# Weight parts of a feed-forward stage: low halves by accumulating DMA, no copies of parts in HBM, weight loads from GpSimd's queue

## The chip, the cores and the metric

The kernel runs on one core of one Trainium2 chip. The metric is the device time of one execution in microseconds (us). A core has five engines that run side by side and wait for one another through semaphores: TensorE (PE in the profile; its weight loads are PEld), VectorE (DVE), ScalarE (ACT), GpSimd (POOL) and SyncE (SP). SP computes nothing here; it issues DMAs. POOL computes and can also issue DMAs on a queue of its own. TensorE's clock is granted by a throttle, and the profile shows the granted share.

## The reference, cut to what matters

```python
x: (1, 2048, 512);  H = 32 heads of Dh = 16;  window W = 8, dilation 2;  F = 1792
qkv = x @ wqkv                                  # (512, 1536)
logits[s, w] = q[s] . k[s - 2*w] / 4            # masked where s - 2*w < 0
a = (sum over w of softmax(logits) * v[s - 2*w]) @ wo
b = (gelu(x @ w_gate) * (x @ w_up)) @ w_down    # (512, 1792) twice, (1792, 512)
g = sigmoid(sum(x * gate_w))
out = g * a + (1 - g) * b
```

Everything is float32.

## The kernel before

**Parities and stages.** Because the dilation is 2, even and odd tokens never meet in the attention. The 2048 tokens are two parities (`par`) of 1024 tokens, each of two blocks of 512. TensorE first does the projections to q, k, v of both parities (`project`, three blocks of columns `cb`). Then comes the feed-forward part of parity 0 (`ffn(0)`), 14 chunks `f` of 128 hidden channels, its end (`finish(0)`: the output projection with `wo`, added to the feed-forward sums, and the output), and then the same for parity 1. The sliding attention is VectorE's work: a generator (`attention`) yields it in small pieces, and `pull(budget)`, called between TensorE's products, takes as many pieces as the budget pays for. An attention unit is 128 channels of one parity, 8 in all; each has 8 pieces of scores (L238, L239), a softmax and 8 pieces of mixing (L273, L277, L278, L279).

**Two parts per operand.** TensorE takes the rounded type fp32r. To keep float32's precision each operand is a high part (the value rounded by a ScalarE copy) and a low part (value minus high part), and each product is three matmuls: high by high, high by low, low by high. `split` (L64 to L69) makes both parts: L68 on ScalarE, L69 a subtraction on VectorE or GpSimd.

**Seven products in place of eight.** `gate_up` computes gate and up of two token blocks with a Strassen-like scheme: seven products of sums. The x operands are a11, a12, a22 and the sums s1 to s4 (`sums`); the weight operands are b11, b21, b22 and the differences t1 to t4 (`combine`, three VectorE subtractions a chunk, L344). `product` is six matmuls of 128x512 (L381), so 42 a chunk; `down` multiplies hidden activations by `w_down` (L420), six matmuls a piece, 16 pieces for each pair of chunks. VectorE adds two products to saved copies (L390), multiplies gate by up (L394) and, in parity 0, makes the low part of the hidden activations (L397); in parity 1 GpSimd makes that.

**Where the weight parts come from.** In parity 0, `fetch` loads a chunk's raw weights from SP's queue, `combine` forms t1 to t4, and `operands` splits each of the seven 128x256 operands: high on ScalarE, low on GpSimd. Each pair of parts is also written to HBM (`WS`), and parity 1 only reads them back. `down_w` does the same with `w_down` (tiles `d`, HBM copies `DS`). `operands(f + 1)` is advanced a step at a time (`idle`, `next(more)`) while chunk f computes.

**The x operands of parity 1** are made at the end of `ffn(0)` (`operands_1`): x is loaded again, and ScalarE and GpSimd split a11, a12, a22 and the four sums.

**Order.** A scheduler with a timeline of its own fixes, when the program is built, the order of the instructions on each engine; on the chip each engine runs its list in that order.

The kernel lays its HBM scratch for the attention's output (`OS`) so that `channels` reads it with four DMAs of 64 KB per half unit.

Of the kernel before, what the change touches and what calls it, by code (L numbers as in the profile page):

```python
# [16 lines left out]
P = 128  # L17
# [16 lines left out]
OPS = ("b11", "t1", "t2", "b21", "b22", "t3", "t4")  # L34
# [3 lines left out]
def tile_gated_mix(ctx: ExitStack, tc: tile.TileContext, xt, wqkv, wff, wo, out):  # L38
# [6 lines left out]
    BUFS = {"A": 16, "S": 16, "w": 14, "d": 4, "raw": 2, "t": 1, "hh": 6, "hl": 6, "c": 4, "s": 3,  # L45
            "r": 2, "rt": 4, "p": 4, "lg": 2}
    COLS = {"w": 2 * WQ, "c": 2 * WQ, "d": 1024, "t": 1024, "raw": WT}

    def tl(tag, dt=F32):
        return pool.tile([P, COLS.get(tag, 512)], dt, name=tag, bufs=BUFS[tag])  # L50

# [20 lines left out]
    KS, VS, QS, OS, WS, DS = {}, {}, {}, {}, {}, {}  # L72
    for par in range(2):
# [6 lines left out]
        for u in range(NU):  # L80
            for half in range(2):
                OS[par, u, half] = dram.tile([32, 4, BT * P], F32, name=f"os{par}{u}{half}")


    early = iter(["c", "rt"] * 99)
    X, WC = {}, {}

    def load_xk(kc, blk, first=False):
        hi, lo = tl("A", F32R), tl("A", F32R)
        X[0, blk, kc] = hi, lo  # L90
        for a, n in ((0, P), (P, 512 - P)) if first else ((0, 512),):
            raw = tl(next(early))
# [4 lines left out]
    def load_cb(cb, kc, eng, tag=None):  # L97
        hi, lo = tl("w", F32R), tl("w", F32R)
        WC[cb, kc] = hi, lo
        raw = tl(tag or "c")  # L100
        if cb == 1:
            n = 2 * WQ
            for hh in range(2):
                nc.sync.dma_start(raw[:, hh * WQ:(hh + 1) * WQ], wqkv[hh, 2, :, kc * WQ:(kc + 1) * WQ])
        else:
            n = 512
            nc.sync.dma_start(raw[:, :n], wqkv[cb // 2, kc // 2, :, kc % 2 * 512:kc % 2 * 512 + 512])
        return lambda: split(eng, hi[:, :n], lo[:, :n], raw[:, :n])

    def sums(par, kc, a, b, eng, put, eng2=None):  # L110

        t = tl("t")
        s1, s2, s3, s4 = t[:, :512], t[:, 512:], b[:, :512], a[:, 512:1024]
        eng.tensor_tensor(s1, b[:, :512], b[:, 512:1024], op=OP.add)
        eng.tensor_tensor(s2, s1, a[:, :512], op=OP.subtract)
        eng.tensor_tensor(s3, a[:, :512], b[:, :512], op=OP.subtract)
        eng.tensor_tensor(s4, a[:, 512:1024], s2, op=OP.subtract)
        for n, s in (("s1", s1), ("s2", s2), ("s4", s4), ("s3", s3)):
            hi, lo = tl("S", F32R), tl("S", F32R)
            split(eng2 or eng, hi, lo, s)  # L120
            put(n, hi, lo)
            yield

    def raw_pair(par, kc):
        ab = []
        for blk in range(2):
            raw = tl("raw")
            nc.sync.dma_start(raw[:, :1024].rearrange("p (a c) -> p a c", a=2), xt[2 * par + blk, :, kc:kc + 3:2, :])
            ab.append(raw)
        return ab  # L130

    XOP, nxt = {}, {}

    def load_x1():
        for kc in range(2):
            a, b = raw_pair(1, kc)
            for blk, raw in ((0, a), (1, b)):
                for i in range(2):
                    if blk == 1 and (kc, i) != (1, 1):
                        d = tl("d", F32R)  # L140
                        hi, lo = d[:, :512], d[:, 512:]
                    else:
                        hi, lo = tl("hh", F32R), tl("hl", F32R)
                    X[1, blk, kc + 2 * i] = hi, lo
                    split(nc.vector, hi, lo, raw[:, i * 512:(i + 1) * 512])

    def operands_0():
        for kc in range(2):
            a, b = raw_pair(0, kc)
            for _ in sums(0, kc, a, b, nc.vector, lambda n, hi, lo: XOP.__setitem__((n, kc), (hi, lo))):  # L150
                pass
# [3 lines left out]
    def operands_1(first):  # L155
        for kc in range(2):
            a, b = raw_pair(1, kc) if kc else first
            for n, raw in (("a11", a[:, :512]), ("a12", a[:, 512:1024]), ("a22", b[:, 512:1024])):
                nxt[n, kc] = tl("A", F32R), tl("A", F32R)
                split(nc.gpsimd, *nxt[n, kc], raw)  # L160
                yield
            yield from sums(1, kc, a, b, nc.vector, lambda n, hi, lo: nxt.__setitem__((n, kc), (hi, lo)), nc.gpsimd)
# [100 lines left out]
    def mix(par, u):  # L263
# [4 lines left out]
        tb = pool.tile([P, NP, UC], F32, name="tb")  # L268
        for jj in range(NP):
            if jj % BT == 0:  # L270
                o = pool.tile([P, BT, UC], F32, name="o")
# [7 lines left out]
            nc.vector.tensor_tensor(o[:, jj % BT], prod[:, 0], prod[:, 1], op=OP.add)  # L279
            yield 1.4  # L280

            if jj % BT == BT - 1:
                nc.vector.transpose(tb[:, jj + 1 - BT:jj + 1].rearrange("p t c -> p (t c)"),
                                    o.rearrange("p t c -> p (t c)"))
                for a in range(4):
                    nc.sync.dma_start(OS[par, u, jj // BT][:, a], tb[32 * a:32 * a + 32, jj + 1 - BT:jj + 1])
# [44 lines left out]
    RAW = {}  # L331

    def fetch(f):
        raw = tl("raw")
        nc.sync.dma_start(raw[:, :1024], wff[f, :, :1024])
        RAW[f] = [raw]

    def combine(f):

        raw, t = RAW[f][0], tl("t")  # L340
        quart = raw[:, :1024].rearrange("p (a b) -> p a b", a=4)
        b11, b21, b12, b22 = (raw[:, i * 256:(i + 1) * 256] for i in range(4))
# [313 lines left out]
```

## Time and profile before

| what | value |
|---|---|
| three timed runs | 678.10, 679.92, 680.22 us; median 679.92 |
| profiled execution | 680.39 us; its span on the core is 678.6 us |
| busy, share of the span | PE 93%, PEld 76%, DVE 86%, ACT 46%, POOL 35% |
| matmuls | 2839 |
| mean granted clock of TensorE | 0.967 |
| DMA traffic | 136.46 MB, 201 GB/s over the span; SP's queue 63.8% of 16 engines' time, POOL's 0.1% |

How to read it: the profile is of one execution, 1.8 us longer than its span and within 0.1% of the median. Busy time counts instructions under way, waits left out. A row of groups such as "L277 DVE TENSOR_TENSOR ... x64 | 59.0, 922" says that 64 instructions of line 277 took 59.0 us together, 922 ns each on average. Matmuls overlap in the pipeline: in a full stretch they start every 0.227 us (88 in 20 us), though each is listed at about 0.4 us.

### The profile page before, as it was taken

Reading aid. Unit: us, or ns where it says so; the run is one execution under the profiler, and the core shown is the slowest. Engines: PE = TensorE matmul, PEld = TensorE weight load, DVE = VectorE, ACT = ScalarE, POOL = GpSimd, SP = SyncE. Lnnn points to the kernel's source line nnn. Section 1 sums busy time; section 2 is a strip of 40 time slices with the busy share of each in tenths; the row PEclk is TensorE's granted clock in tenths of the full one; section 3 lists DMA queues with packets and bytes.
Section 4 is the critical chain, followed back from the end, with each engine's and each line's share of the span. In section 5 each row is a group of like instructions: output and inputs, shape, how many; then the busy total and the mean of one; then the engine's idle time right before and its main releaser. Section 6 shows DMA issues by size and latency. Waiting matters only on the chain.

```text
span 678.6 us, 8894 instructions
## 1 busy us (share of the span) xinstructions
PE 631.2 (93%) x2839; PEld 512.9 (76%) x2839; DVE 584.4 (86%) x714; ACT 313.8 (46%) x601; POOL 236.1 (35%) x198
## 2 busy tenths in 40 slices
PE   8998999996799979997989849999999999999997
PEld 6888998874587758875868637888777888887785
DVE  5439899879999999989999988998999999989432
ACT  4424442245446455655454564234434644454562
POOL 5204014066737364634471760023122221224220
PEclk9999999998799989998998978999999999999999
DMA  8885755597966665675457587776566766544163
GB/s 254 269 253 172 247 156 187 172 300 250 310 235 218 243 229 171 234 252 208 156 191 224 159 225 158 249 234 218 179 187 197 214 196 197 185 124 127 36 104 124
DMA packets 116046, 136.46 MB, mean 201 GB/s; under 512 B 42400, under 2 KB 68640, under 8 KB 116000
## 3 DMA queue, kind: packets, MB, share of 16 engines
q1 hardware_dynamic: 115488, 135.84, 63.8%
q8 instruction: 22, 0.36, 0.2%
q14 instruction: 24, 0.20, 0.1%
q0 software_dynamic: 512, 0.07, 0.1%
HBM read 81.80 MB, written 54.07 MB: 200 GB/s over the span
## 4 chain that ended last, share of the span: by engine, by line
DVE 41%; PE 38%; DMA 7%; issue 6%; ACT 4%; SPq 1%; POOL 1%; DVEq 0%; POOLq 0%; ACTq 0%
PE p L381 21%; DVE prod L273 6%; PE p L420 6%; PE acc L420 5%; DVE prod L238 5%; DVE prod L277 4%; DVE lg L239 4%; DMA raw<-xt 4%; PE acc L557 3%; PE p L557 3%; DVE t L344 3%; DVE c L394 3%; DVE c L390 2%; DVE prod L278 2%; DVE o L279 2%
## 5 line engine op out<-in xcount | busy, mean ns | idle before, releaser
L381 PE MATMUL p<-S,w 128*128 128x512 f32 x672 | 176.6, 406 | 10.2 <-DVE c L390 4.1
L381 PEld LDWEIGHTS p<-S,w 128*128 128x128 f32 x672 | 130.8, 195 | 42.8 <-DVE c L390 4.5
L381 PE MATMUL p<-A,w 128*128 128x512 f32 x504 | 135.6, 407 | 16.2 <-DVE c L390 16.0
L381 PEld LDWEIGHTS p<-A,w 128*128 128x128 f32 x504 | 97.1, 194 | 42.4 <-DVE c L390 20.0
L397 POOL TENSOR_TENSOR hl<-c,hh 128x512 fp32r<-128x512 f32 x28 | 44.7, 1595 | 168.5 <-ACT hh L396 141.4
L238 DVE TENSOR_TENSOR prod<-k,q 128x1024 f32<-128x1024 f32 x64 | 86.8, 1356 | 11.5 <-DMA q<-qs 10.6
L273 DVE TENSOR_TENSOR prod<-v,lg 128x1024 f32<-128x1024 f32 x64 | 81.5, 1273 | 6.7 <-DMA v<-vs 5.3
L420 PE MATMUL p<-d,hh 128*128 128x512 f32 x224 | 71.7, 405 | 10.5 <-ACT p L414 10.4
L239 DVE TENSOR_REDUCE lg<-prod 128x64 f32<-128x1024 f32 x64 | 77.7, 1214 | 1.1
L69 POOL TENSOR_TENSOR w<-t,w 128x256 fp32r<-128x256 f32 x56 | 58.4, 1056 | 48.2 <-ACT w L68 38.5
L396 ACT ACTIVATE hh<-c 128x512 fp32r<-128x512 f32 x56 | 35.3, 631 | 80.3 <-DVE c L394 80.0
L69 POOL TENSOR_TENSOR w<-raw,w 128x256 fp32r<-128x256 f32 x42 | 43.0, 1034 | 63.8 <-ACT w L68 60.6
L277 DVE TENSOR_TENSOR prod<-prod 128x512 f32<-128x512 f32 x64 | 59.0, 922 | 1.3
L420 PEld LDWEIGHTS p<-d,hh 128*128 128x128 f32 x224 | 43.0, 194 | 22.0 <-ACT p L414 11.8
L420 PE MATMUL acc<-d,hh 128*128 128x512 f32 x224 | 57.7, 394 | 0.7 <-ACT hh L396 0.7
L420 PEld LDWEIGHTS acc<-d,hh 128*128 128x128 f32 x224 | 41.8, 188 | 11.7 <-ACT hh L396 2.4
L394 DVE TENSOR_TENSOR c<-c 128x512 f32<-128x512 f32 x56 | 44.6, 796 | 5.2 <-ACT c L482 4.8
L385 ACT ACTIVATE s<-p 128x512 f32<-128x512 f32 x56 | 32.8, 593 | 26.2 <-PE p L381 26.2
L390 DVE TENSOR_TENSOR c<-p,s 128x512 f32<-128x512 f32 x56 | 38.0, 681 | 8.0 <-PE p L381 7.8
L420 PE MATMUL p<-d,hl 128*128 128x512 f32 x112 | 42.9, 394 | 0.0
L429 ACT ACTIVATE rt<-p 128x512 f32<-128x512 f32 x48 | 28.6, 595 | 29.4 <-PE p L420 28.0
L177 PE MATMUL p<-w,A 128*128 128x512 f32 (+2 forms) x192 | 38.5, 345 | 2.9 <-ACT w L68 1.1
(125 smaller groups left out, 1002.0 us busy)
## 6 DMA issues: line engine op xcount, KB each, us to landing
ws<-w SPq DMA_DIRECT2D x98, 256.0 KB, 2.9
w<-ws SPq DMA_DIRECT2D x98, 256.0 KB, 2.7
raw<-wff SPq DMA_DIRECT2D x14, 512.0 KB, 5.0
ds<-d SPq DMA_DIRECT2D x14, 512.0 KB, 3.9
d<-ds SPq DMA_DIRECT2D x14, 512.0 KB, 4.5
raw<-xt SPq DMA_DIRECT2D x12, 512.0 KB, 5.4
k<-ks SPq DMA_DIRECT2D x8, 512.0 KB, 5.0
q<-qs SPq DMA_DIRECT2D x8, 512.0 KB, 6.3
```

Of the source, the lines that this page charges most:

```text
L69: eng.tensor_tensor(lo, raw, hi.bitcast(F32), op=OP.subtract)
L177: nc.tensor.matmul(ps[:, :cn], a[:, t], w[:, c0:c0 + cn], start=(kc == 0 and n == 0), stop=(kc == KC - 1 and n == 2))
L238: nc.vector.tensor_tensor(prod, k[:, jj:jj + W, :], q[:, jj, None, :].to_broadcast([P, W, UC]), op=OP.mult)
L239: nc.vector.tensor_reduce(lg[:, jj].rearrange("p w h -> p (w h)"), prod.rearrange("p w (h d) -> p (w h) d", d=DH), axis=AX.X, op=OP.add)
L273: nc.vector.tensor_tensor(prod.rearrange("p w (h d) -> p w h d", d=DH), v[:, jj:jj + W, :].rearrange("p w (h d) -> p w h d", d=DH), lg[:, ...
L277: nc.vector.tensor_tensor(prod[:, :4], prod[:, :4], prod[:, 4:], op=OP.add)
L381: nc.tensor.matmul(ps, w_, a_, start=(start and kc == 0 and n == 0), stop=(kc == 1 and n == 2), skip_group_check=True)
L390: nc.vector.tensor_tensor(c, ps, s, op=OP.add)
L394: nc.vector.tensor_tensor(ge, ge, up, op=OP.mult)
L397: eng.tensor_tensor(hl_, ge, hh_.bitcast(F32), op=OP.subtract)
L420: nc.tensor.matmul(pp, a[:, ts], w, start=(i == 0 and n == 0 and gr == 0), stop=(i == 1 and n == 2), skip_group_check=True)
L557: nc.tensor.matmul(pa, a, b, start=False, stop=(u == NU - 1 and n == 2), skip_group_check=True)
```

## The change

- `operands` no longer splits seven operands one by one. Raw weights and differences now lie side by side in one tile `raw` of eight quarters, in the order t1, t2, b11, b12, b22, t3, t4, b21, and are handled in two groups (t1, t2, b11: 768 columns; b22, t3, t4, b21: 1024 columns). For each group ScalarE writes the negated high part into the place of the low part, a DMA from GpSimd's queue adds the raw values onto it (`accum_op=OP.add`), and ScalarE writes the high part. This is done in both parities; `WS` and `DS` are gone, so parity 1 fetches raw weights, runs `combine` and splits `w_down` (on GpSimd) like parity 0.
- Weights, `w_down` and `wo` are loaded from GpSimd's queue; the outputs of parity 0 leave from it as well.
- The x operands of parity 1 are made at the beginning (`load_x1`): VectorE makes the sums and all the low parts, GpSimd's queue writes the parts to HBM (`keep`, 28 DMAs of 256 KB), and in the last chunk of parity 0 the queue reads them back (`operands_1`, 14 DMAs of 512 KB). `sums` works in place.
- `OS` is laid out so that one DMA reads a half unit in `channels`; VectorE's last addition of a mix piece writes `o` in another order.
- Buffers are regrouped (`g0`, `g1` for the weight parts, pairs in `A` and `S`).

```diff
+GROUPS = (("t1", "t2", "b11"), ("b22", "t3", "t4", "b21"))
+QUARTS = ("t1", "t2", "b11", "b12", "b22", "t3", "t4", "b21")
...
+    def keep(n, kc, hi, lo):
+        x = XS[n, kc] = dram.tile([P, 1024], F32, name=f"x{n}{kc}")
+        nc.gpsimd.dma_start(x[:, :512], hi.bitcast(F32))
+        nc.gpsimd.dma_start(x[:, 512:], lo.bitcast(F32))
     def load_x1():
...
+            for n, x in sums(a, b):
+                hi, lo = pair("S")
+                split(nc.vector, hi, lo, x)
+                keep(n, kc, hi, lo)
...
-    def operands_1(first):
+    def operands_1(n):
         for kc in range(2):
-            a, b = raw_pair(1, kc) if kc else first
-            for n, raw in (("a11", a[:, :512]), ("a12", a[:, 512:1024]), ("a22", b[:, 512:1024])):
-                nxt[n, kc] = tl("A", F32R), tl("A", F32R)
-                split(nc.gpsimd, *nxt[n, kc], raw)
-                yield
-            yield from sums(1, kc, a, b, nc.vector, lambda n, hi, lo: nxt.__setitem__((n, kc), (hi, lo)), nc.gpsimd)
+            t = tl("A" if n[0] == "a" else "S", F32R)
+            nc.gpsimd.dma_start(t.bitcast(F32), XS[n, kc])
+            XOP[n, kc] = t[:, :512], t[:, 512:]
...
-            nc.vector.tensor_tensor(o[:, jj % BT], prod[:, 0], prod[:, 1], op=OP.add)
+            two = [prod[:, i].rearrange("p (b c) -> p b c", b=4) for i in range(2)]
+            nc.vector.tensor_tensor(o[:, :, jj % BT], *two, op=OP.add)
...
     def fetch(f):
-        raw = tl("raw")
-        nc.sync.dma_start(raw[:, :1024], wff[f, :, :1024])
-        RAW[f] = [raw]
+        raw = RAW[f] = tl("raw")
+        r = raw.rearrange("p (a c) -> p a c", c=QW)
+        q = wff[f, :, :1024].rearrange("p (a c) -> p a c", c=QW)
+        nc.gpsimd.dma_start(r[:, 2::5], q[:, :2])
+        nc.gpsimd.dma_start(r[:, 3:5], q[:, 2:])
+    def fetch_d(f):
+        RD[f] = tl("r")
+        nc.gpsimd.dma_start(RD[f], wff[f, :, 1024:])
     def combine(f):
...
-        sub(t[:, :512].rearrange("p (a b) -> p a b", a=2), quart[:, 2:], quart[:, 0::2])
-        sub(t2, b22, t1)
-        sub(t4, b21, t2)
+        sub(r[:, 0:6:5], r[:, 3:5], r[:, 2:4])
+        sub(q["t2"], q["b22"], q["t1"])
+        sub(q["t4"], q["b21"], q["t2"])
-    def operands(par, f):
+    def operands(f):
...
-            if par:
-                nc.sync.dma_start(w[:, :512].bitcast(F32), WS[f][i])
-            else:
-                split(nc.gpsimd, w[:, :256], w[:, 256:512], RAW[f][n])
-                nc.sync.dma_start(WS[f][i], w[:, :512].bitcast(F32))
+            raw = RAW[f][:, (0, 4)[i] * QW:][:, :n]
+            nc.scalar.activation(lo, raw, AF.Copy, scale=-1.0)
+            nc.gpsimd.dma_start(lo.bitcast(F32), raw, accum_op=OP.add)
             yield
+            nc.scalar.activation(hi, raw, AF.Copy)
+            yield
-    def down_w(par, f):
+    def down_w(f):
         d = WD[f] = tl("d", F32R)
-        if par:
-            nc.sync.dma_start(d.bitcast(F32), DS[f])
-            return
-        rd = tl("r")
-        nc.sync.dma_start(rd, wff[f, :, 1024:])
-        DS[f] = dram.tile([P, 1024], F32, name=f"ds{f}")
-        split(nc.gpsimd, d[:, :512], d[:, 512:], rd)
-        nc.sync.dma_start(DS[f], d.bitcast(F32))
+        split(nc.gpsimd, d[:, :512], d[:, 512:], RD.pop(f))
...
     def channels(par, u, half):
         o = tl(("r", "rt")[half])
-        src = OS[par, u, half].rearrange("i a (t b j) -> b i (a t) j", t=BT, b=4)
-        for b in range(4):
-            nc.sync.dma_start(o[32 * b:32 * b + 32].rearrange("p (m j) -> p m j", j=32), src[b])
+        nc.sync.dma_start(o, OS[par, u, half].rearrange("b i a c -> (b i) (a c)"))
...
-                    nc.sync.dma_start(out_v[2 * jj + par, :, c], r[:, c])
+                    (nc.sync if par else nc.gpsimd).dma_start(out_v[2 * jj + par, :, c], r[:, c])
```

More of the change, by code (lines that the diff above doesn't have):

```diff
@@ L1 @@
 from contextlib import ExitStack
-from itertools import chain
 import numpy as np
@@ L110, in sums, with columns, of @@
[L110 to L121, printed above, removed]
-            yield
+    def columns():
+        def of(*tags):
+            for tag, n in tags:
+                t = tl(tag, F32R)
+                yield from (t[:, i * 2 * WQ:(i + 1) * 2 * WQ] for i in range(n))
+        cb0 = of(("g1", 4), ("g1", 4))
+        cb1 = of(("g0", 3), ("g0", 3), ("hh", 1), ("hl", 1))
+        for cols in (cb0, cb1):
+            for _ in range(KC):
+                yield next(cols), next(cols)
+        cols = of(("g1", 4))
+        for _ in range(2):
+            yield next(cols), next(cols)
+        yield pair("d")
+        yield tl("c", F32R), tl("c", F32R)
@@ L446, in piece, with anew @@
                 down(par, *s)
+        def anew(*names):
+            if not par and f == FC - 1:
+                for n in names:
+                    operands_1(n)
         X_ = bank("p")
@@ L484, in gate_up, with ahead, again @@
         late.append(last)
+    AGAIN = {}
+    def ahead():
+        combine(0)
+        AGAIN[0] = operands(0)
+        for _ in range(2):
+            yield next(AGAIN[0])
+    def again():
+        yield from AGAIN.pop(0)
+        yield from load_o((2, 3), (tl("c", F32R)[:, :512] for _ in range(4)))
+        fetch(1)
+        yield
+        combine(1)
     def ffn(par):
@@ L598, in tile_gated_mix @@
     combine(0)
-    ops = operands(0, 0)
-    for i in range(6):
-        next(ops)
+    for _ in operands(0):
+        pass
     combine(1)
```

197 lines of the change are left out of this document (120 added, 77 removed).

## The prediction

> **What bounds the kernel now.** I read the page first, then busy time by stage, then TensorE's waits, then the order of time on VectorE and GpSimd. The page gives TensorE 93% and VectorE 86%, but shares over the span mix stages, so I cut it at four points: the first feed-forward matmul (144), where the clock recovers and the end of parity 0 is under way (400), the first product of parity 1 (435.3), and the last mix of the attention (633.5).
>
> ```profile
> 144.00:400.00 256.00, 224.74 (x910) 177.54 (x908) 246.75 (x285) 133.51 (x268) 144.90 (x123) 0.94 0.67 222
> 400.00:435.30 35.30, 28.72 (x112) 22.68 (x113) 29.80 (x44) 17.83 (x29) 5.44 (x4) 0.82 0.68 187
> 435.30:633.50 198.20, 196.73 (x845) 157.88 (x844) 188.25 (x229) 87.45 (x144) 47.48 (x30) 1.00 0.59 186
> 633.50:678.60 45.10, 40.97 (x178) 32.95 (x176) 12.30 (x19) 20.80 (x36) 6.43 (x5) 1.00 0.44 100
> ```
>
> The columns are window, length, PE, PEld, DVE, ACT, POOL busy, granted clock, DMA share, GB/s. Matmuls at full pace start every 0.227 us. Parity 0's stage (call it B) has 910, which need 207 us, and lasts 256; VectorE is busy 246.75, 96%. So VectorE bounds B. Parity 1's stage (D) needs 192 us for 845 matmuls, lasts 198.2, and VectorE is at 95%: both engines are nearly full. The short end of parity 0 (C) and the tail (E) are mostly TensorE's.
>
> ```profile
> PE p L381 <- DVE c L390: 19.0, 6, 4.8
> PE p L420 <- ACT p L414: 10.4, 2, 7.7
> ```
>
> These are TensorE's longest waits from 144 to 420. They are few, but after gaps of 3 us and more the clock row falls to a half: the window 248 to 256 has a granted clock of 0.57, 316 to 324 as well, 398 to 413 has 0.54, while 436 to 640 has 1.00. That is why B has 3.6 matmuls a us and D 4.3.
>
> Why is VectorE full in B with about the same work? Because its instructions are longer there:
>
> ```profile
> 621.22 1.68 DVE L277 TENSOR_TENSOR prod<-prod 128x512 f32<-128x512 f32 x1
> 622.93 1.40 DVE L278 TENSOR_TENSOR prod<-prod 128x256 f32<-128x256 f32 x1
> 626.44 0.68 DVE L277 TENSOR_TENSOR prod<-prod 128x512 f32<-128x512 f32 x1
> 627.64 0.42 DVE L278 TENSOR_TENSOR prod<-prod 128x256 f32<-128x256 f32 x1
> ```
> ```profile
> 620.01 2.34 POOL L397 TENSOR_TENSOR hl<-c,hh 128x512 fp32r<-128x512 f32 x1 [1.90 <-ACT hh L396]
> 622.30 1.75 POOL L69 TENSOR_TENSOR w<-r,w 128x512 fp32r<-128x512 f32 x1
> ```
>
> The same VectorE subtraction or addition takes 0.68 us with GpSimd idle and 1.68 beside a GpSimd TENSOR_TENSOR. Taking each line's median as its undisturbed price (1224 ns for L238 and L273, 693 for L277, 424, 292, 684, 680 for L397, 414 and 688 for L344), these lines are 67 us longer than count times median; over all VectorE rows it is 76 us: 6 before 144, 50 in B, 2 in C, 17 in D and 1 in E. GpSimd's TENSOR_TENSOR time there is 21, 143, 5, 44 and 7 us, so 0.35 us is lost per us of it.
>
> **The change, part by part.**
>
> 1. *GpSimd's splits of weights go* (98 x 1.03 to 1.06 = 101 us), and its 14 splits of the second parity's x (23 us). In B there remain 14 splits of `d` (24.7) and `wo` (about 7): 32 of 143 us. Loss on VectorE in B: 50 to 50 x 32/143 = 11, a gain of 39 us of VectorE time.
>
> 2. *Splits of `d` come to parity 1*: 13 x 1.78 = 23 us of GpSimd in D. Loss there from 17 to 17 x 67/44 = 26 us.
>
> 3. *`combine` also in parity 1*: at medians 0.688 + 2 x 0.414 = 1.5 us. By the changed program's order ten stand in D: +15 us of VectorE; three more stand in C, where VectorE waits for nobody.
>
> 4. *Moved x operands.* Eight sums and eight low parts (16 x 0.69 = 11 us) go to VectorE before 144, out of 37 us that it has idle there; GpSimd's row then waits behind `keep`. In the order, two mixes (2.63 each) slip from there into B; B loses the eight sums (5.5 us) and two pieces of scores (4.9), which slip into D with one mix (+7.5). The 28 `keep` writes are 7.3 MB more beside 32 MB moved before 144 (0.72 of the engines' time): I put the first stage at 145 us instead of 144, with bounds 144 (hidden by 140 us of TensorE work) and 151 (7.3 MB at the 220 GB/s of that window is 33 us, a fifth of it exposed).
>
> 5. *ScalarE.* Per chunk two pieces of 768 and two of 1024 columns. From 412 ns at 256 and 628 at 512 they are 0.84 and 1.06: 3.8 us, against 7 x 0.412 = 2.9 in parity 0 and nothing in parity 1. With 0.63 for `d` that is 13 x 4.4 = 57 us more in D, from 87 to 145 of 228: room, but pieces of 1.06 us stand ahead of the copies that TensorE waits for (L385, L451, L414).
>
> 6. *GpSimd's queue.* Five DMAs per chunk. The only rows are the 4 KB ones at the start, 0.52 us each. At that price a chunk costs GpSimd 2.6 + 1.8 (+ 3.2 for L397 in parity 1) = 7.6 of 15 us. The upper end is the point where the queue fills: 2.0 us each. I take about 1 us, hidden. Each adding DMA also waits for ScalarE's negated copy; behind it in GpSimd's list stand the next splits of `d` and, in parity 1, L397, whose result `down` needs only with the next pair of chunks, some 15 us later. SP loses 322 of 580 issues; its queue bounds nothing now and that is worth nothing.
>
> 7. *The accumulating DMA* is in no row. Two per chunk, 896 KB, are due a chunk later, 15 us. The nearest rows: 256 KB from SBUF lands in 2.9 us, 512 KB in 3.9 (parts to HBM). Lower end: two such copies, under 9 us, hidden. Upper end: four times those, 30 us a chunk, which would double the feed-forward. I take the lower, because the bytes per chunk (2.5 MB even if an addition reads twice) fit into 17 us at 150 GB/s, and 222 are moved now. The Trainium skill speaks against it: Collectives: The Full Stack, under "The bandwidth ceiling", has an adding DMA at half a copy's rate because of two source reads; by that the two would take an estimated 12 to 14 us in place of under 9. No row here shows it, and it would still be inside the chunk.
>
> **The sum.** B: VectorE 246.75 - 39 - 5.5 - 4.9 + 5.3 = 203 us, now under TensorE's 207. With both full, D's ratio holds (198.2 / 192 = 1.03): 214 us, **-42**. C: without the 8 us wait for L414 (it stood behind splits of the sums on ScalarE) and its half clock: 30, **-5**. D: VectorE 188.25 + 9 + 15 + 7.5 = 220; at B's 96% that is 228 us, **+30**: VectorE is late next here, and parity 1 looks like parity 0 now. E: by the order three mixes are left when the last chunk begins its additions, and TensorE has got on meanwhile; some 156 matmuls remain where 178 did, partly beside them: 33, **-12**. Start: **+1**. Together 145 + 214 + 30 + 228 + 33 = 650 of span, plus the 1.8 us that the profiled execution has outside it, less 0.5 that it stands above the median: **651 us, 4% faster**.
>
> **Rivals.**
>
> *Slower: writing descriptors disturbs VectorE as GpSimd's additions do.* 70 DMAs per parity at 1 us and 0.35 lost per us are 25 us more on VectorE in B (then 228, so 237 long) and 23 in D (252 long): 651 + 23 + 24 = 698. It decides when the loss passes 28 us. Against it: around 10 us GpSimd issues DMAs without pause, and VectorE's additions with two SBUF inputs keep their price:
>
> ```profile
> 9.73 0.69 DVE L69 TENSOR_TENSOR A<-rt,A 128x512 fp32r<-128x512 f32 x1
> 10.02 1.03 POOL L78 DMA_DIRECT2D ks<-zero  x2
> 10.56 0.69 DVE L69 TENSOR_TENSOR A<-c,A 128x512 fp32r<-128x512 f32 x1
> ```
>
> The Trainium skill (SBUF — State Buffer, "Who interferes with whom") infers the same: an addition takes the shared read side, descriptors the write side. These DMAs have 8 rows, the new ones 128, so 0.08 stays. With it goes the like case of late weights, as in 7, at 17 us a chunk and above (from 685 on): 0.08.
>
> *The adding DMAs do not show and D is not VectorE's:* if the additions in D fill gaps, D is 212 and E 37, and the time is 639. VectorE's 5% idle in D speaks against more than that. 0.17.
>
> *ScalarE's long pieces make TensorE wait.* One extra wait of 0.7 us a chunk in 28 chunks is 20 us: 671. For it: 16.5 us of waits for ScalarE in B and C already. Against: in D none over 1 us. 0.14.
>
> *The change only moves the loss:* B gains less because the scheduler's order is tight, D loses as much: within 0.3% of the old time, 0.04, a little under it 0.04.
>
> **How the numbers follow.** The forecast of 651 (645 to 662) has 0.45, and the cases add up to faster 0.80, same 0.04, slower 0.16; 0.3% is about what a measurement of this kernel tells from no change. The range reaches from the low bounds (144 + 210 + 30 + 205 + 38 + 1.3 = 628, where D is no longer than its matmuls nearly) to the first rival's 698; about 0.05 stays below and 0.1 above.
>
> **What would show it.** Right: VectorE's L322 (the old L277) near 0.7 us in parity 0, stages of 214, 30 and 228 us, the granted clock at 1.0 in B and below it in D. Wrong: VectorE additions over 1 us with only DMAs on GpSimd; DMA_DIRECT2D on POOL over 2 us; TensorE waiting for a weight part `g`, or for ScalarE, more than 15 us in all.

## The result, and the profile after

The changed kernel takes **689.48 us** (median of 4 runs, 686.82 to 691.58), the kernel before 679.27 beside it: ratio 1.015, 95% interval 1.011 to 1.019, so 1.5% slower. The forecast was 651 us, 4% faster. The profiled execution took 686.82 us, its span is 685.0.

The windows of the kernel after, cut at the same events as those of before (first feed-forward matmul, where the end of parity 0 is under way, first product of parity 1, last mix); columns as before:

```profile
0.00:158.00 158.00, 144.37 (x799) 124.58 (x800) 119.75 (x154) 60.15 (x131) 43.21 (x67) 0.98 0.78 243
158.00:380.00 222.00, 211.36 (x894) 167.85 (x893) 201.36 (x277) 137.41 (x218) 80.61 (x96) 0.99 0.65 169
380.00:414.90 34.90, 31.74 (x129) 24.97 (x128) 33.29 (x42) 21.72 (x34) 19.45 (x20) 0.95 0.72 236
414.90:662.20 247.30, 226.51 (x940) 178.22 (x939) 225.06 (x280) 146.84 (x233) 116.97 (x113) 0.98 0.52 133
662.20:685.00 22.80, 19.04 (x83) 15.11 (x81) 7.98 (x14) 5.01 (x9) 0.00 (x0) 1.00 0.33 115
```

| stage | before | forecast | after |
|---|---|---|---|
| A, start | 144.0 | 145 | 158.0 |
| B, parity 0 | 256.0 | 214 | 222.0 |
| C, end of parity 0 | 35.3 | 30 | 34.9 |
| D, parity 1 | 198.2 | 228 | 247.3 |
| E, tail | 45.1 | 33 | 22.8 |
| span | 678.6 | 650 | 685.0 |

The middle (B and C) is 34 us shorter, the start 14 longer, the end (D and E) 27 longer. VectorE's busy column was forecast well: 203 for B (201.36 came), 220 for D (225.06). What was not forecast is the idle time beside it: in D VectorE is idle for 22 us and TensorE for 21. TensorE's longest waits, of the kernel after:

```profile
PE p L426 <- DVE c L435: 12.2, 9, 3.9
PE p L222 <- ACT z L241: 6.9, 3, 4.7
PE p L426 <- ACT p L501: 4.9, 3, 2.7
PE p L426 <- ACT s L430: 4.3, 3, 2.4
PE acc L465 <- ACT hh L441: 3.5, 2, 3.1
```

They are shorter than before, but elsewhere. Taken by stage, all listed waits of TensorE add up to 13.6 us in A (3.9 before), 13.7 in B and C (37.7 before), and 20.7 in D and E (1.3 before). So the waits went out of the middle and came back in the first and the last part.

What they hang on has changed, too. The page follows the chain of work that ended last back from the end, and gives each kind of step its share of the span; first before, then after:

```profile
DVE 41%; PE 38%; DMA 7%; issue 6%; ACT 4%; SPq 1%; POOL 1%; DVEq 0%; POOLq 0%; ACTq 0%
```
```profile
PE 28%; DVE 25%; DMA 19%; issue 18%; POOL 5%; ACT 4%; SPq 1%; DVEq 0%; POOLq 0%; ACTq 0%
PE p L426 17%; DMA raw<-wff 6%; DMA g<-raw 5%; PE acc L465 5%; DVE prod L318 4%; DMA raw<-xt 4%; PE p L465 4%; DVE prod L283 3%; DVE raw L395 3%; DVE lg L284 3%; DVE c L439 2%; DVE prod L322 2%; DVE prod L323 2%; DVE c L435 2%; PE p L642 2%
```

Work of VectorE and TensorE made up 79% of that chain before and makes up 53% now. Transfers went from 7% to 19%; the loads of raw weights have 6% of it and the adding DMAs 5%, some 75 us together. ("Issue" is time for which the profile shows no wait.)

**The start.** The first 100 us of before, then of after:

```profile
0.00:60.00 60.00, 56.06 (x278) 46.23 (x279) 31.82 (x45) 26.70 (x49) 18.31 (x27) 1.00 0.81 244
60.00:100.00 40.00, 40.00 (x333) 39.93 (x332) 37.69 (x42) 14.79 (x52) 2.94 (x3) 1.00 0.67 207
```
```profile
0.00:60.00 60.00, 55.66 (x276) 45.76 (x277) 32.92 (x47) 24.07 (x42) 28.96 (x52) 1.00 0.95 306
60.00:100.00 40.00, 30.71 (x240) 29.28 (x239) 38.56 (x42) 17.08 (x46) 9.96 (x10) 0.98 0.71 222
```

The DMA engines go from 0.81 to 0.95 of their time in the first 60 us, and the matmuls that are missing are missing behind that: 240 from 60 to 100, where 333 stood. One 5 us gap there can be followed back over three engines, in the orders of time of VectorE, GpSimd (twice), VectorE again and ScalarE:

```profile
59.19 0.69 DVE L150 TENSOR_TENSOR raw<-raw 128x512 f32<-128x512 f32 x1 [13.47 <-DMA raw<-xt]
```
```profile
81.54 0.73 POOL L384 DMA_DIRECT2D raw<-wff  x1 [32.47 <-DVE S L76]
```
```profile
82.84 2.56 POOL L76 TENSOR_TENSOR g<-raw,g 128x512 fp32r<-128x512 f32 x2
```
```profile
83.67 5.32 DVE L283 TENSOR_TENSOR prod<-k,q 128x1024 f32<-128x1024 f32 x1
```
```profile
84.83 0.20 ACT L258 ACTIVATE en<-z 128x8 f32<-128x8 f32 x1
95.02 1.06 ACT L411 ACTIVATE g<-raw 128x1024 fp32r<-128x1024 f32 x1 [9.99 <-DVE raw L395]
```

VectorE waits 13 us for x, whose load leaves SP at 50.7 us and lands 8.4 us later, and makes the sums behind that. The first weight load has to wait for them, because they hold its `raw` buffer (`S`, L76): it leaves at 81.5 us, where it leaves at 71.4 in e2 below, without the x writes. It has landed by 85.5, but `combine` (L395) starts only at 92.7, and without a wait: it stands in VectorE's list behind pieces of scores, one of which takes 5.32 us where the next takes 1.23. That one runs beside four splits of GpSimd (82.8 to 87.9), which stand behind the late load in GpSimd's list. So ScalarE, whose list has the weights' copy L411 ahead of copies out of PSUM, stands for 10 us; TensorE waits 4.7 us of them for L241, and its clock is at a half for the 6.8 us behind that. Over the whole of A, TensorE's waits are 9.7 us more than before, and 6.8 us at half the clock lose an estimated 3.4 more: 13 of the 14 us.

**GpSimd and VectorE.** From the page of after:

```profile
L412 POOL DMA_DIRECT2D g<-raw x56 | 50.7, 906 | 139.4 <-ACT g L411 124.5
L395 DVE TENSOR_TENSOR raw<-raw 128x256 f32<-128x256 f32 (+1 forms) x84 | 49.2, 588 | 23.9 <-DMA raw<-wff 23.5
L322 DVE TENSOR_TENSOR prod<-prod 128x512 f32<-128x512 f32 x64 | 50.3, 786 | 1.0
```

Issuing an adding DMA costs GpSimd 0.9 us, the addition L322 (old L277) has come from 922 to 786 ns on the mean (from 0.99 to 0.69 us in B, where the splits of the groups went; 0.88 in D), and a new wait stands in VectorE's list: 23.5 us before `combine`, for the raw weights. How it comes about, first in GpSimd's order, then in VectorE's:

```profile
203.26 0.75 POOL L384 DMA_DIRECT2D raw<-wff  x1 [8.31 <-ACT p L501]
203.99 0.60 POOL L385 DMA_DIRECT2D raw<-wff  x1
```
```profile
202.36 1.22 DVE L283 TENSOR_TENSOR prod<-k,q 128x1024 f32<-128x1024 f32 x1
207.37 0.69 DVE L395 TENSOR_TENSOR raw<-raw 128x512 f32<-128x512 f32 x1 [3.79 <-DMA raw<-wff]
```

The load leaves GpSimd only when VectorE is about to need it; it takes 3.5 us to land, and VectorE's list has nothing else in that place.

### The profile page after: what moved, and what is told of

The parts are those of the page before. It is cut to its first block, busy times and chain, and to the rows that moved or that the text cites. A ratio compares the mean times of both kernels' runs of the same rounds, so it can differ in the third digit from the quotient of the medians.

```text
span 685.0 us, 8454 instructions
## 1 busy us (share of the span) xinstructions
PE 633.0 (92%) x2839; PEld 510.7 (75%) x2839; DVE 587.4 (86%) x764; ACT 371.1 (54%) x623; POOL 260.2 (38%) x294
## 4 chain that ended last, share of the span: by engine, by line
PE 28%; DVE 25%; DMA 19%; issue 18%; POOL 5%; ACT 4%; SPq 1%; DVEq 0%; POOLq 0%; ACTq 0%
PE p L426 17%; DMA raw<-wff 6%; DMA g<-raw 5%; PE acc L465 5%; DVE prod L318 4%; DMA raw<-xt 4%; PE p L465 4%; DVE prod L283 3%; DVE raw L395 3%; DVE lg L284 3%; DVE c L439 2%; DVE prod L322 2%; DVE prod L323 2%; DVE c L435 2%; PE p L642 2%
## 5 line engine op out<-in xcount | busy, mean ns | idle before, releaser
L426 PE MATMUL p<-S,g 128*128 128x512 f32 x672 | 174.9, 403 | 11.8 <-ACT p L501 4.9
L426 PEld LDWEIGHTS p<-S,g 128*128 128x128 f32 x672 | 128.9, 193 | 45.6 <-ACT p L501 6.5
L426 PE MATMUL p<-A,g 128*128 128x512 f32 x504 | 130.5, 396 | 12.0 <-DVE c L435 11.3
L426 PEld LDWEIGHTS p<-A,g 128*128 128x128 f32 x504 | 93.8, 188 | 37.9 <-DVE c L435 15.7
L412 POOL DMA_DIRECT2D g<-raw x56 | 50.7, 906 | 139.4 <-ACT g L411 124.5
L441 ACT ACTIVATE hh<-c 128x512 fp32r<-128x512 f32 x56 | 35.4, 632 | 64.3 <-DVE c L439 64.0
L395 DVE TENSOR_TENSOR raw<-raw 128x256 f32<-128x256 f32 (+1 forms) x84 | 49.2, 588 | 23.9 <-DMA raw<-wff 23.5
L411 ACT ACTIVATE g<-raw 128x1024 fp32r<-128x1024 f32 (+1 forms) x56 | 53.1, 947 | 15.8 <-DVE raw L395 15.0
L384 POOL DMA_DIRECT2D raw<-wff x28 | 21.2, 758 | 100.2 <-DVE S L76 32.5
L76 POOL TENSOR_TENSOR d<-r,d 128x512 fp32r<-128x512 f32 x28 | 46.4, 1663 | 27.2 <-ACT d L75 23.9
L465 PEld LDWEIGHTS acc<-d,hh 128*128 128x128 f32 x224 | 42.7, 192 | 14.9 <-ACT hh L441 5.1
L414 ACT ACTIVATE g<-raw 128x1024 fp32r<-128x1024 f32 (+1 forms) x56 | 52.9, 944 | 0.0
L322 DVE TENSOR_TENSOR prod<-prod 128x512 f32<-128x512 f32 x64 | 50.3, 786 | 1.0
## 6 DMA issues: line engine op xcount, KB each, us to landing
raw<-wff POOLq DMA_DIRECT2D x56, 256.0 KB, 3.5
r<-wff POOLq DMA_DIRECT2D x28, 256.0 KB, 3.1
xs<-S POOLq DMA_DIRECT2D x16, 256.0 KB, 5.0
```

The lines of the kernel that those rows point to most:

```text
L322: nc.vector.tensor_tensor(prod[:, :4], prod[:, :4], prod[:, 4:], op=OP.add)
L395: sub = lambda o, a, b: nc.vector.tensor_tensor(o, a, b, op=OP.subtract)
L411: nc.scalar.activation(lo, raw, AF.Copy, scale=-1.0)
L412: nc.gpsimd.dma_start(lo.bitcast(F32), raw, accum_op=OP.add)
L414: nc.scalar.activation(hi, raw, AF.Copy)
L426: nc.tensor.matmul(ps, w_, a_, start=(start and kc == 0 and n == 0), stop=(kc == 1 and n == 2), skip_group_check=True)
```

## The experiments

Each kernel was timed beside the kernel before; ratios are to that, with the 95% interval. "First product" is the end of A, "middle" B and C, "end" D and E, from the profiled execution. For the changed kernel they are 158.0, 256.9 and 270.1 us; for the kernel before 144.0, 291.3 and 243.3. Two limits hold for all of them. The stages are those of one execution, and the executions of one kernel spread over 1 to 8 us, so a difference of 5 us in a stage is near the limit of what they tell. And an edit gives the scheduler another program, so the order of instructions changes with it.

My theory after the result: three separate losses, namely the traffic of the x writes at the start, the work that parity 1 has to do again, and waits for the raw weights. The rival: the same work is only pushed back and forth.

**e1: loads from SP.**

```diff
-        nc.gpsimd.dma_start(r[:, 2::5], q[:, :2])
+        nc.sync.dma_start(r[:, 2::5], q[:, :2])
```
(likewise the other half, and in `fetch_d` and `fetch_o`)

> The changed kernel, with the loads of raw weights, w_down and wo issued from SP's queue again; all else stays on GpSimd's. In the changed kernel VectorE stands still for 18.7 us in the feed-forward stages (10.4 in parity 0, 8.3 in parity 1) because combine waits for raw<-wff. Theory: the loads are late because they stand in GpSimd's list behind adding DMAs that wait for ScalarE. Then that wait falls under 6 us, and the time from 689 to 672 to 680 us. Rival: the scheduler puts combine too early for any queue, or the landing itself is slow; then the wait stays over 12 us and the time between 685 and 693.

Measured: 700.5 us, ratio 1.032 (1.026 to 1.037). VectorE's wait and the longest of SP's queue:

```profile
DVE raw L395 <- DMA raw<-wff: 43.6, 19, 6.6
```
```profile
SPq L384 <- DMA g<-raw: 153.4, 25, 17.8
```

The wait nearly doubled, and the time is over what either theory allowed. A load can be issued only when the adding DMA has read its buffer, and on SP's queue, too, it waits for that. That it holds up the attention's transfers behind it in SP's list is not shown: VectorE's waits for them stay small in this run (3.4 us for `v`). GpSimd's queue was the better place for the loads.

**e2 and e3: without the x writes, and without the early sums as well.**

```diff
     def keep(n, kc, hi, lo):
+        if (n, kc) != ("a11", 0):
+            return
```
(all 14 reads take that one pair; e3 also drops the sums, splits and `keep` in `load_x1`)

> The changed kernel without 26 of its 28 writes of parity 1's x operands to HBM; the 14 later loads all read the one pair that is still written, so parity 1 computes with wrong x operands. VectorE's early sums and splits stay. In the changed kernel the first feed-forward product starts at 158 us, 14 later than before. Theory A: those 7 MB of writes crowd the DMA engines (busy 0.90 to 0.98 of the first 60 us) and delay x, q and k; then the first product starts at 144 to 149 and the time is 676 to 682. Theory B: the early sums hold the two raw tiles, so that the loads after them come late; then it starts at 155 or later and the time is 686 to 692.

> As the run without the writes, and also without the eight early sums of parity 1 and their splits (the sums are not computed at all). Theory A (traffic): no better than the run without the writes, within 3 us at the first product. Theory B (the sums hold the raw tiles and VectorE): the first product comes at 144 to 148 here and not there; the time is 672 to 680. If it still starts after 153, the cause is neither, and the order of the tiles' reuse for the weights' first loads remains.

Measured: e2 673.11 us, ratio 0.991 (0.988 to 0.994), first product 143.1, middle 262.8, end 268.3. So without the writes the late start is gone, all 15 us of it, as theory A had it. e3: 666.29 us, 0.982 (0.978 to 0.984), first product 142.1, middle 255.9, end 266.9. The early sums and splits, 11.6 us of VectorE in A, cost 7 us more, and these show in the middle, where VectorE does what it did not get done of the attention in A.

**e4: `d` by an adding DMA too**, so that GpSimd makes no splits in `down_w`.

```diff
-        split(nc.gpsimd, d[:, :512], d[:, 512:], RD.pop(f))
+        raw = RD.pop(f)
+        nc.scalar.activation(d[:, 512:], raw, AF.Copy, scale=-1.0)
+        nc.gpsimd.dma_start(d[:, 512:].bitcast(F32), raw, accum_op=OP.add)
+        nc.scalar.activation(d[:, :512], raw, AF.Copy)
```

> The changed kernel with the low part of w_down made as the other weights' (ScalarE's negated copy, then an adding DMA) in place of GpSimd's 28 subtractions. In the changed kernel VectorE loses 57 us beside 112 us of GpSimd's TENSOR_TENSOR, 0.51 a us, and 0.6 us beside 78 us of GpSimd's DMA instructions alone. Theory (parity 1 lost because GpSimd's subtractions of d came to it, and VectorE is what bounds both parities): 46 us of subtractions less give VectorE 24 us, and the time falls to 668 to 678. Rival (adding DMAs and their queue are the cost, the more of them the worse): 28 more adding DMAs, 687 us or more.

Measured: 684.67 us, 1.009 (1.005 to 1.012), between the two theories, a miss for both. VectorE's busy time fell by 13.5 us in the middle and 5.7 at the end, but the middle grew from 256.9 to 261.7 and only the end fell, to 264.6. VectorE's wait for raw weights rose to 29.6 us, and transfers have 24% of the chain that ended last, where they had 19%. VectorE's work alone no longer sets the middle.

**e5: parity 1's weight parts written to HBM and read back**, as before the change, but made by adding DMAs.

```diff
+            if par:
+                nc.sync.dma_start(w[:, :2 * n].bitcast(F32), WSG[f, i])
...
             nc.scalar.activation(hi, raw, AF.Copy)
+            nc.sync.dma_start(WSG[f, i], w[:, :2 * n].bitcast(F32))
```

> The changed kernel, but parity 0 writes its weight parts (groups and d) to HBM from SP, 17 MB in all, and parity 1 reads them back from SP, with no subtractions, copies, adding DMAs or splits there; nothing is left out of the computation. Theory A: parity 1 and the tail are longer than before (270 us against 243) because VectorE has 13 combines more (84 groups of subtractions become instructions in parity 1) and GpSimd 13 splits more beside VectorE. Then they come back to 243 to 250 us, the first two stages stay at 158 and 257 to 262, and the total is 660 to 672. Theory B: those stages are long because of the late start of the attention's work, which is pushed into parity 1 whatever the weights do. Then parity 1 and the tail stay at 265 or more, and the total is 683 to 692. Theory C: the writes hold up the adding DMAs of parity 0: the middle stage grows past 270 us.

Measured: 667.6 us, 0.980 (0.975 to 0.985); first product 157.1, middle 263.7, end 245.3. Theory A holds: the end is back. The middle is 7 us longer, and its last part is where that shows: from the first output matmul of parity 0 to parity 1 it takes 34.4 us, 23.2 in the changed kernel, and TensorE waits 6.3 us of them for the high parts of the attention's output. Why those come late there was not followed; e9 has the same writes of weight parts and no such delay.

**e6: the load of the chunk after next asked for at the beginning of a chunk.**

```diff
+            if f + 2 < FC:
+                fetch(f + 2)
             down_w(f)
```

> The changed kernel with the load of the chunk after next asked for at the beginning of a chunk (as before the change) and no longer between the two groups' parts, still from GpSimd; nothing is left out. Theory A: VectorE's 23.5 us of waits for raw<-wff come from the place of the load in GpSimd's list, and they are on the path in the middle stage and in parity 1, where VectorE is the busiest engine. Then they fall under 10 us and the total to 670 to 680. Theory B: the load waits for its buffer (raw has two, and the adding DMA reads it last), so asking earlier changes nothing: the waits stay at 20 us or more and the total within 4 us of 687, or the waiting load holds up what is behind it on GpSimd and the total is over 691.

Measured: 686.8 us, 1.010 (1.007 to 1.014); VectorE's wait 23.9 us. Theory B: `raw` has two buffers, and GpSimd waits 30.3 us in this kernel (28.2 in the changed one) for the adding DMA to have read one. Asking earlier changes nothing.

**e7 and e8: the x writes listed later** (e8 with e5's edit).

```diff
-                keep(n, kc, hi, lo)
+                SK.append((n, kc, hi, lo))
...
-    operands_0()
     project(0, 1)
     keep_x1()
+    operands_0()
```

> The changed kernel with the same 28 writes of parity 1's x parts, but none of them asked for before the second projection of parity 0 is listed; the sums of parity 0 follow behind them. Nothing is left out. Theory A: the late first product (158 us against 144) comes from these 7.3 MB standing beside the loads and stores of the first 60 us, when the DMA engines are at 0.90 to 0.98. Then, with the same bytes later, the first product comes at 143 to 148 and the total is 672 to 679. Theory B: the bytes cost the same wherever they stand before 144 us: the first product stays at 154 to 160, the total at 683 to 692.

> The two preceding edits together (late writes of the x parts, parity 1's weight parts from HBM). If the start and parity 1 are separate losses and each edit mends its own, the gains add: first product at 143 to 150, parity 1 and tail 243 to 250, total 645 to 660, faster than both kernels. If they are one loss, that is the same work pushed back and forth, the total is that of the better of the two, 660 to 680.

Measured: e7 690.25 us, 1.016 (1.012 to 1.020), first product 157.2; e8 670.72 us, 0.989 (0.984 to 0.995), 156.8. These runs tell nothing on the question: the scheduler still put all 16 writes of `S` into the first 70 us, as the DMA issues of both show. Where the line stands in the source is not where it runs.

**e9: e5, and parity 1's x operands made late as before the change.** Of the change there remain the adding DMAs in parity 0, the loads and parity 0's outputs on GpSimd's queue, the regrouped buffers and the layout of `OS`.

```diff
-            t = tl("A" if n[0] == "a" else "S", F32R)
-            nc.gpsimd.dma_start(t.bitcast(F32), XS[n, kc])
+            a, b = raw_pair(1, kc) if kc else first
+            for n, raw in (("a11", a[:, :512]), ("a12", a[:, 512:]), ("a22", b[:, 512:])):
+                nxt[n, kc] = pair("A")
+                split(nc.gpsimd, *nxt[n, kc], raw)
```
(and the same for the four sums; no sums and no `keep` in `load_x1`)

> The changed kernel with parity 1's weight parts written to HBM in parity 0 and read back (as in e5), and also with parity 1's x operands made late as before the change: loaded again during the last chunk of parity 0, summed on VectorE, split by GpSimd; no early sums and none of the 28 writes. So of the change only the adding DMAs of parity 0 stay, with the loads on GpSimd. Nothing is left out. Theory A: the early x operands cost the start 13 to 16 us by their writes, and the late ones cost at the end of parity 0 at most half of that. Then the first product comes at 142 to 146 instead of 157, and the total is 650 to 660 (e5: 668). Theory B: what the start gains comes back at the end of parity 0, where 14 splits and 8 sums stand between two parities: parity 1's first product stays at 418 to 424, and the total at 664 to 672.

Measured: **651.94 us, 0.961 (0.958 to 0.964)**, faster than both kernels. Its three stages:

```profile
0.00:141.80 141.80, 139.95 (x800) 121.86 (x801) 107.36 (x146) 56.34 (x123) 32.58 (x39) 1.00 0.80 243
141.80:401.70 259.90, 242.02 (x1022) 189.49 (x1020) 239.85 (x314) 160.96 (x256) 99.87 (x99) 1.00 0.88 283
401.70:648.60 246.90, 239.32 (x1021) 190.47 (x1020) 208.60 (x255) 107.89 (x182) 62.66 (x45) 1.00 0.49 167
```

The start is 15 us shorter than in e5, and the end of parity 0 did not take it back (theory B there): from the first output matmul of parity 0 to parity 1 it is 23.8 us, against 23.2 after, 34.4 in e5 and 23.5 before. That its time is the forecast of 651 us almost to the microsecond is chance, for it is another kernel. The clock is at 1.00 throughout, and transfers have 10% of the chain that ended last. VectorE's busy time in the middle, 276.55 us in the kernel before, is 239.85.

**e10 and e12: the kernel before, with 28 writes added**, in e10 of parity 1's parts as they are made, in e12 of parity 0's sums, which are ready later.

```diff
                     split(nc.vector, hi, lo, raw[:, i * 512:(i + 1) * 512])
+                    for part in (hi, lo) * 2:
+                        x = dram.tile([P, 512], F32, name=f"x{len(nxt)}")
+                        nxt[len(nxt)] = x
+                        if len(nxt) < 29:
+                            nc.gpsimd.dma_start(x, part.bitcast(F32)[:, :512])
```

> The kernel before the change, with 28 writes of 256 KB (7.3 MB) of parts of parity 1's x from GpSimd right behind their splits, to places in HBM that nobody reads; nothing else is changed. Theory A: the bytes beside the loads and stores of the first 60 us are the cause of the late start, without any of the change's other work. Then the first product moves from 144 to 153 to 158 and the total rises by 8 to 14 us, to 686 to 692. Theory B: the bytes are harmful only together with the sums, the splits and the waiting buffers of the changed kernel. Then the first product stays under 148 and the total under 683.

> The kernel before the change with 28 writes of 256 KB from GpSimd as in e10, but of the parts of parity 0's x sums, which are ready only from about 66 us; nobody reads them. The DMA share from 60 to 140 us is 0.52 to 0.71 there, against 0.70 to 0.87 up to 60. Theory A: the bytes cost time where the DMA engines are full (up to 60 us), and are nearly free behind that. Then the first product stays at 144 to 147 and the total at 678 to 685. Theory B: 7.3 MB cost the same wherever they stand ahead of the first product: total 690 to 702, as in e10.

Measured: e10 698.45 us, 1.031 (1.028 to 1.034), first product 149.6, middle 290.9, end 252.6 (its profiled execution has a span of 693.0); e12 690.89 us, 1.018 (1.014 to 1.021), first product 149.3, middle 285.6, end 254.1. One window of e10, one of e12:

```profile
0.00:60.00 60.00, 53.37 (x244) 43.18 (x245) 21.72 (x37) 23.62 (x40) 28.78 (x52) 0.97 0.96 321
```
```profile
60.00:100.00 40.00, 36.09 (x282) 35.37 (x281) 25.62 (x30) 11.66 (x43) 11.83 (x17) 0.96 0.93 310
```

The writes alone make the kernel before 2 to 3% slower. Of the sizes, e10 is a miss for both theories, and e12's time is at the edge of theory B's range. The first product moves only 5 us, not the 14 of the changed kernel, where the early sums and the `raw` buffers come on top. VectorE (fifth column) loses 10 us of its 31.82 up to 60 us in e10, and 12 of its 37.69 from 60 to 100 in e12. The DMA engines are at 0.96 and 0.93 there, and VectorE waits for transfers: in e10 13.8 us for staging buffers to be written out (`qs<-s`, 3.0 before), in e12 13.1 for `q` (10.6 before) and 7.3 for raw weights (1.3 before). The end is 9 and 11 us longer in these two. In e12 the first 16 writes left from 48 to 62 us and the last 12 from 71 to 79, so 7.3 MB are not free behind 60 us either; they fill 0.67 up to 0.93. Part of the loss can be the order: the kernel before has a piece of scores ahead of the first sum in VectorE's list, e10 four sums ahead of the first piece of scores. No run holds the order fixed.

**e11: e9 with `d`'s low part in parity 0 by an adding DMA.** The edit is that of e4.

> The kernel of e9 with the low part of d in parity 0 made by an adding DMA as well, so that in the middle stage GpSimd has almost no TENSOR_TENSOR left. Theory A: VectorE is still what the middle stage waits for; 14 splits of about 1.75 us beside it cost it some 12 us, and the total falls by 6 to 12 us against e9. Theory B: with the groups' splits gone the middle stage is set by TensorE and by waits between engines: the total is within 3 us of e9, as e4 gave 5 us for 28 such splits.

Measured: 661.6 us, 0.974 (0.971 to 0.978), slower than e9 by 10 us, a miss for both theories. VectorE's busy time in the middle fell by 12.7 us, and the middle grew from 259.9 to 263.9. Transfers have 23% of the chain that ended last, 10% in e9. Of GpSimd's waits these are new or longer:

```profile
POOL raw L374 <- ACT g L407: 33.4, 3, 11.7
POOL hl L448 <- issue: 32.9, 4, 11.7
POOL r L379 <- DMA d<-r: 27.2, 10, 7.1
```

The first is a load behind a copy of ScalarE, the second has no releaser in the profile, and the third is the load of `r`, which waits until the adding DMA has read it. VectorE's wait for raw weights came from 6.7 to 14.1 us. That the end, whose code is the same, also grew by 6 us is not explained by these runs.

**e13 and e14: one of e5's two steps each.** e13 reads only `d` back, e14 only the groups.

> The changed kernel with only d's parts written to HBM in parity 0 and read back in parity 1 (7.3 MB); the groups are made again in parity 1 as in the change. It measures the step that brought 13 splits of d on GpSimd to parity 1. By the prediction's size VectorE gets 9 us back there: parity 1 and the tail go from 270 to 259 to 263, the total to 677 to 683. Rival: the splits hide in parity 1, where VectorE also has idle time: within 4 us of the changed kernel, 685 to 692.

> The changed kernel with only the groups' parts written to HBM and read back (25.7 MB); d is split again in parity 1. It measures the combine on VectorE, the long copies on ScalarE and the adding DMAs of parity 1 together. If the two steps add up to what e5 gained (21 us) and d is worth 8, it gains 13: total 673 to 678. If the groups are nearly all of it (the waits for raw and the subtractions go, and VectorE has room for the d splits' disturbance), the total is 666 to 671.

| end (D and E), us; ratio with interval | groups made again | groups read back |
|---|---|---|
| `d` split again | 270.1; 1.015 (1.011 to 1.019) | 255.1; 0.995 (0.993 to 0.997) |
| `d` read back | 265.3; 1.012 (1.005 to 1.018) | 245.3; 0.980 (0.975 to 0.985) |

The groups cost the end 15 to 20 us, `d` 5 to 10, together 25. The times agree with the rival of e13: `d` read back alone gains 2.5 us (687.02), and 7 with the groups read back as well (674.66 to 667.6). That it hides behind the groups' waits fits this and is not shown.

## Why the prediction was wrong

The mechanism it argued for is there: L322 came to 0.69 us in B, as forecast, and in e9, where the x operands of parity 1 are made late and its weight parts come from HBM as before, the middle is 31 us shorter. (The loads, outputs and buffers that go with the adding DMAs are part of those 31.) What failed is step 4, the price of the moved x operands (1 us forecast, 14 measured), and the time that the sum allowed for waits beside full engines. The sum was 35 us too low, 13 of it in A, 13 in B and C, 9 in D and E.

1. *GpSimd's splits go.* Right in VectorE's work (203 forecast in B, 201.36 came). Over the whole kernel VectorE's additions beside a GpSimd TENSOR_TENSOR lost 57.5 us to 112 us of it, 0.51 per us, where 0.35 was taken from the trace before.
2. *`d` in parity 1*, a loss in D of 26 us where 17 stood: about 28 by the same working, and the end is 4.8 to 9.8 us shorter without these splits (e13 and its partners). Right, as far as the spread lets one tell.
3. *`combine` in parity 1*, 15 us: its 33 subtractions in D took 21.69 us, 7 more. All of the groups' work there, waits and copies included, costs the end 15 to 20 (e14 and its partners).
4. *Moved x operands*, +1 us, bounds 144 and 151: 158 came. **This step failed most.** It counted the bytes against TensorE's 140 us of work, as if only the first product mattered, and took VectorE's 37 idle us as room for the sums. The runs put 15 us of the start on the writes beside the early sums (e2), 7 of the total on the sums (e3), and 20 on writes added to the kernel before (e10, its new order included). Two things were missing. With the DMA engines at 0.95, transfers that VectorE needs for the attention and the sums land late, and its work slips. And the `raw` buffer that the late sums hold delays the first weight load and GpSimd's splits behind it, from which the chain above leads to a 5 us gap of TensorE.
5. *ScalarE*, from 87 to 145 us in D: 146.84 came. Its pieces are 0.95 us on the mean. The rival built on them, 20 us of waits, came in part: TensorE waits 12.7 us for ScalarE in D and E, 0.2 before, and 29.2 in all, over the 15 that were named as a sign of being wrong (but 18.6 stood there before). That the long pieces are the cause is not shown: ScalarE waits for VectorE in D as well, 24.0 us before L441 alone.
6. *GpSimd's queue*, about 1 us a DMA: 0.54 to 0.91. The price was right, the cover was not: the load waits for its buffer, and VectorE for the load (23.5 us, of which 4.8 in A, 10.4 in B and C, 8.3 in D). The step looked for who stands behind the adding DMA, and named the `d` splits and the low part of the hidden activations; the load of the chunk after next stood there as well.
7. *The adding DMA*: near the lower end in landing time, but not hidden. 512 KB landed in 4.9 us and 384 KB in 4.7, 9.6 for both where under 9 were allowed; TensorE waits for no `g` in the changed kernel. The half rate that the Trainium skill gives for the adding DMAs of ReduceScatter (Collectives: The Full Stack, "The bandwidth ceiling") does not show in these landing times: a plain 512 KB load of `wo` takes 4.7 us in the same trace. Under e9's HBM writes the adding DMAs take 8.1 and 7.6, and a plain load of 256 KB 6.4 where it took 3.5. But the step asked only when the parts are due. The addition also keeps `raw` occupied until it has read it, and so it stands on the way of the load of the chunk after next, with 5% of the chain.

*The sum.* "With both full, D's ratio holds" took B to 214 on the grounds that neither engine would wait much. D of before has 1.3 us of waits of TensorE; the middle after has 13.7. In e4 and e11 less work for VectorE did not shorten the middle, which fits waits and not work, though both runs add DMAs to GpSimd's list. For D the sum had 8 us of idle time beside VectorE's 220 us of work; 22 came beside 225. "E: 33" and "C: 30": E came as 22.8, as the attention ended later. C lost its long wait (7.7 us for L414; the longest is 3.0 now) and holds 129 matmuls where 112 stood, at the same length. What sets each of the middle's remaining waits is not settled.

*Rivals.* Descriptor writing does not disturb VectorE: its additions beside GpSimd's DMA instructions alone (some 150, about 77 us of overlap) lost 0.6 us in all. The Trainium skill's inference (SBUF — State Buffer, "Who interferes with whom") agrees with that, for DMAs of 128 rows too. So that mechanism for "slower" is not what made it slower. The other one, late weights, is the nearest in size (from 685 us, at 17 us a chunk; parity 1's chunks took 16.6, and 14.9 before) but not in kind: the parts `g` do not keep TensorE waiting, the raw weights keep VectorE waiting. "The change only moves the loss", 0.08 in all, comes nearest in its picture, though not in its time: waits moved from the middle to both ends.

## What to carry to other kernels

An engine's idle time early in a kernel is no room if its later work could have come forward into it: price moved work by what it displaces, and moved bytes by every load that shares the DMA engines, not by the one stage that they stand in. When a step gets cheaper, take the stage's new length from work plus waits, and look for the buffer whose reader has become slower to start. A change with several parts is best judged one part at a time: here one was worth 31 us in the middle, and two others cost more than that at the start and the end.

## What the runs showed of the hardware

- An accumulating DMA of 512 KB within SBUF lands in 4.9 us (median of 28), about as a plain load of 512 KB does (4.7, four of them) in the same trace.
- GpSimd's issue of a DMA of 128 rows takes 0.54 to 0.91 us on the mean, one of 8 rows 0.52, and VectorE's additions beside it lost 0.6 us over some 77; beside GpSimd's TENSOR_TENSOR they lost 0.35 us (before) and 0.51 us (after) per us of it. One piece of scores took 5.32 us beside four of these, 1.23 alone.
- 28 writes of 256 KB, 7.3 MB that nobody reads, came with 13 to 20 us more in a kernel whose source is otherwise the same (its order of instructions is not). SP's queue alone takes 63.8% of the DMA engines' time in that kernel over the span; while the writes ran, the engines were at 0.93 to 0.96.
